# Regrouping the token blocks of an attention-plus-bilinear-FFN kernel: seven groups instead of eight, seven-product matmuls in five of them

## The chip, the cores and the metric

The kernel runs on one core of a Trainium2 chip. The metric is the device time of one execution in microseconds, the median of several runs. The engines of a core work side by side and wait for each other through semaphores: TensorE (PE in the profile; its weight loads are PEld), VectorE (DVE), ScalarE (ACT), GpSimd (POOL) and SyncE (SP), which here only issues transfers. GpSimd and ScalarE issue transfers too.

## The reference

Two layers are computed one after the other. The first is a causal linear attention with a decay per head, on q, k, v of shape (4 batches, 8 heads, 768 positions, 64). In blocks of the sequence it is

```
intra = einsum('bhic,bhjc->bhij', qb, kb) * Dmask      # lam ** (i - j), lower triangle
intra = einsum('bhij,bhjd->bhid', intra, vb)
inter = einsum('bhid,bhde->bhie', qb * lam_pow, kv_state)
out   = intra + inter
kv_state = lam_block * kv_state + einsum('bhsd,bhse->bhde', kb_dec, vb)
```

The second is a bilinear feed-forward layer on the 3072 tokens, x of shape (3072, 512): `a = x @ w_a`, `b = x @ w_b`, `out = (a * b) @ w_out`, with a hidden width of 1536. The output is (3072, 512) in float32.

## The kernel before

**Units and groups.** The 3072 tokens are cut into 24 units of 128 tokens, six to a batch. Attention is computed unit by unit, the feed-forward layer group by group: `GROUPS` (L28) lists how many units each group has. While TensorE runs the feed-forward matmuls of one group, the attention of the units of the next group is woven in between. The order of the weaving is written out by hand: `PLAN` lists, for each group, steps at numbered slots, and the feed-forward routine calls `hook(slot)` at fixed points of its own loop. The instructions are issued in exactly this program order on each engine. An engine works through its queue in order, so a step that waits holds up all that stands behind it on that engine.

**The steps of `PLAN`.** "P" prepares a unit (`prep_k`, L267): k is scaled by a decay vector (on VectorE for the first two units of group 1 on, else on GpSimd), q is scaled on GpSimd, the result is the bf16 tile `qk`; for units in `DMA_T` the SyncE queue then issues a DMA transpose of `qk` to `qkT`; at last `pump` issues the loads of q and k of later units on SyncE, up to a lookahead; then `make_vb` has GpSimd issue the load of v, cast to bf16 on the way. "T" is the transpose on TensorE (`piece_T`, eight 128-column matmuls and one ScalarE copy) for units that are not in `DMA_T`. "S" computes the scores and masks them on VectorE. "V" updates the running state (tile `kvd`) and copies it to SBUF. "O", "O2" and "Q" compute the attention output of one or two units ("Q" with the scores of two more) and copy it to `xT`, the feed-forward input. "W" stores a kept output row block. "TW" computes weight sums (`w_sums`, L467).

**The feed-forward layer.** A plain group (`ffn`, L613) computes, for each of 12 chunks of 128 hidden columns, four matmuls for a and four for b with as many columns as the group has tokens. ScalarE copies a to `a_sb`, VectorE multiplies it with b into `ab`. Then each unit takes twelve 512-column output matmuls (tile `op`). Group 0 is plain and runs the chunks as the weights arrive. A group in `S_GROUPS` runs `ffn_seven` (L492) instead. It treats the products as a 2-by-2 block problem and takes seven block products where the plain way takes eight, at the price of sums: sums of weight blocks `tw` (four VectorE subtractions for each of six parts of 256 hidden columns), sums of input blocks `xs`, and sums after the products, with ScalarE snapshots of PSUM (`s12`, `s5`, `u2`), VectorE sums (`c11`, `c12`, `c22`) and a GpSimd product into `ab`. `SUM_ON_VEC` lists the parts whose `c11` VectorE sums directly; for the others ScalarE copies and GpSimd sums. Before the change only groups of four units run it, and the part loop has six rounds of seven products with four 256-column matmuls each.

**Queues at the start.** SyncE loads q and k of the first four units; GpSimd issues the loads of v of these, then the weights in chunks, `wo_sb` last in six pieces. SyncE then waits, through tiny transfers into `landed`, for pieces 0, 3 and 5 of `wo_sb`, and issues q and k of units 4, 5 and 6 behind them. The load tiles `qf` and `kf` have three buffers each.

**Output.** Rows of the first `KEEP_GROUPS` groups are kept in SBUF and stored by "W" steps later; the others are stored at once. The last unit's output is split into three column ranges so that the last store is small.

Of the kernel before, what the change touches and what calls it, by code (L numbers as in the profile page):

```python
# [22 lines left out]
def _bc(ap, dims):  # L23
# [4 lines left out]
GROUPS = (4, 1, 2, 4, 4, 4, 4, 1)  # L28
# [3 lines left out]
LOOKAHEAD = {9: 2, 10: 1}  # L32
DMA_T = range(7, 24)
KEEP_GROUPS = 3
# [7 lines left out]
S_GROUPS = (3, 4, 5, 6)  # L42
SUM_ON_VEC = {3: (1, 2, 3, 4), 4: (2, 3, 4), 5: (2, 3, 4), 6: (1, 2, 3, 4)}
PLAN = {
    0: [(0, "V", 3), (7, "TW", (0, "dve")), (7, "TW", (1, "dve")), (23, "P", 4), (26, "T", 4),
        (29, "TW", (2, "dve")), (29, "TW", (3, "dve")), (29, "S", 4), (33, "O", 4), (35, "P", 5)],
    1: [(0, "V", 4), (2, "T", 5), (3, "P", 6), (6, "S", 5), (7, "T", 6), (10, "S", 6),
        (10, "TW", (4, "dve", (0,))), (10, "TW", (4, "dve", (1,))), (12, "O2", (5, 6)),
        (12, "TW", (4, "dve", (2,))), (13, "P", 7)],
    2: [(0, "V", 6), (1, "P", 8), (4, "P", 9), (7, "V", 7), (9, "S", 7), (9, "S", 8), (6, "P", 10),  # L50
        (10, "V", 8), (11, "Q", (7, 8, 9, 10)), (12, "P", 11), (12, "V", 9), (13, "O2", (9, 10)),
        (14, "P", 12)],
    3: [(1, "P", 13), (3, "P", 14), (11, "S", 11), (11, "S", 12),
        (7, "P", 15), (12, "P", 16), (14, "P", 17), (17, "P", 18)],
    4: [(6, "P", 19), (9, "P", 20), (13, "P", 21), (16, "P", 22)],
    5: [(6, "P", 23)],
    6: [(13, "O", 23)],
}
for _g, _u in ((3, 11), (4, 15), (5, 19)):
    PLAN[_g] += [(11, "V", _u), (13, "Q", (_u, _u + 1, _u + 2, _u + 3)), (14, "V", _u + 2),  # L60
                 (16, "O2", (_u + 2, _u + 3)), (18, "S", _u + 4)]
    if _g < 5:
        PLAN[_g] += [(19, "S", _u + 5)]
PLAN[3] += [(_s, "W", None) for _s in (9, 9, 9, 10, 10, 10, 10)]
PLAN[2] += [(_s, "TW", (4 + _n // 4, "dve", (_n % 4,)))
            for _n, _s in enumerate((2, 3, 5, 6, 12), 3)]
# [3 lines left out]
def kernel(  # L70
# [60 lines left out]
    def load_x(w, u):  # L131
        b, nb = divmod(u, NB)
        t = ld_pool.tile([128, H, D], F32, name=w + "f", tag=w + "f", bufs=3)
        nc.sync.dma_start(out=t, in_={"q": qr, "k": kr}[w][b, nb])
        raw[u, w] = t
# [31 lines left out]
    def pump():  # L167
        while pending:
            kind, c = pending[0]
            if kind == "after":  # L170
                nc.sync.dma_start(out=landed[:, c:c + 1], in_=wo_sb[0:1, 2 * c + 1, 0:1])
            elif c >= used["u"] + LOOKAHEAD.get(used["u"], 2 if used["u"] > 8 else 3):
                return
            else:
                load_x(kind, c)
            pending.pop(0)
# [76 lines left out]
    def make_ks(u, eng):  # L253
        qk = prep_pool.tile([128, 2, H, D], BF16, name="qk", tag="qk")
        scale(eng, qk[:, 1], raw.pop((u, "k")), lp_k[:, u % NB])
        U[u] = dict(qk=qk, kn=qk[:, 1])
# [10 lines left out]
    def prep_k(u):  # L267
        make_ks(u, "dve" if u < n0 + 2 else "pool")
        make_qs(u, "pool")
        used["u"] = u + 1  # L270
        if u in DMA_T:
            qkT = qkT_pool.tile([128, 2, HP, 128], BF16, name="qkT", tag="qkT")
            nc.sync.dma_start_transpose(
                out=qkT[:].rearrange("p j hp i -> p (j hp) i"),
                in_=U[u]["qk"][:].rearrange("p j h d -> p (j h d)"))
            U[u]["qT"], U[u]["kT"] = qkT[:, 0], qkT[:, 1]
        pump()
# [24 lines left out]
    def masks(u, kq):  # L302
        ms = mask(kq, split=u in (7, 8))
        U[u]["m"] = lambda i, hp: ms[i][:, hp, :]
# [103 lines left out]
    def pieces_O(us, nxt=()):  # L408
        kqs = [score_banks() for u in nxt]
        o_banks(us)  # L410
        for u, kq in zip(nxt, kqs):
            scores(u, kq)
        for u in us:
            inter(u)
        for b in range(2):
            for u in us:
                intra(u, b)
            evac_o(us, b)
        sums(us[-1])
        beside = len(us) == 2 and us[0] >= n0 + 5  # L420
        if beside:
            kv_beside(us[1])
        copy = beside and us[1] % NB < NB - 1
        for n, (u, kq) in enumerate(zip(nxt, kqs)):
            if n == 1 and copy:
                kv_copy(us[1], kv["ps"])
            masks(u, kq)
        if copy and len(nxt) < 2:
            kv_copy(us[1], kv["ps"])
# [37 lines left out]
    def w_sums(i, eng, which=range(4)):  # L467
        if i not in tw:
            tw[i] = wst_pool.tile([128, 4, 2, 256], BF16, name="tw", tag="wst")
        t = tw[i]  # L470
        e = nc.gpsimd if eng == "pool" else nc.vector
        c = slice(256 * i, 256 * i + 256)
        a1, a2, b1, b2 = wa_sb[:, 0:2, c], wa_sb[:, 2:4, c], wb_sb[:, 0:2, c], wb_sb[:, 2:4, c]
        for j in which:
            e.tensor_sub(t[:, j], *((b1, a1), (b2, t[:, 0]), (b2, b1), (a2, t[:, 1]))[j])

    def sums(u):
        g = next(i for i in range(len(GROUPS)) if g_u0[i] <= u < g_u0[i] + GROUPS[i])
        if g not in S_GROUPS or u != g_u0[g] + 3:
            return  # L480
        x = xTs[u][0]
        t = wst_pool.tile([128, 4, 2, 256], BF16, name="xs", tag="wst")
        x11, x12, x21, x22 = (x[:, k:k + 2, c:c + 256] for c in (0, 256) for k in (0, 2))
        nc.vector.tensor_add(t[:, 0], x22, x21)
        nc.vector.tensor_sub(t[:, 1], t[:, 0], x11)
        nc.vector.tensor_sub(t[:, 2], x11, x21)
        nc.vector.tensor_sub(t[:, 3], x12, t[:, 1])
        xs[g] = t
# [3 lines left out]
    def ffn_seven(g, u0, xT, hook):  # L492
# [4 lines left out]
        def bank_of(name):  # L497
            t = ps_bank(name, [128, 2, 256], F32, hold=True)
            return t, (bank["next"] - 1) % 7

        def product(i, ps, w, x, first):
            for f in range(2):
                for k in range(2):
                    nc.tensor.matmul(ps[:, f, :], lhsT=w(k, f), rhs=x[:, k, :],  # L504
                                     start=(first and f == 0 and k == 0), stop=True,
                                     skip_group_check=True)

        def w_of(w_sb, k0, i):
            return lambda k, f: w_sb[:, k0 + k, (2 * i + f) * 128:(2 * i + f + 1) * 128]

        def t_of(j, i):
            return lambda k, f: tw[i][:, j, k, f * 128:(f + 1) * 128]

        x11, x12, x22 = xT[:, 0:2, 0:256], xT[:, 2:4, 0:256], xT[:, 2:4, 256:512]

        def snap(name, ps, bufs, t=None):
            if t is None:
                t = sn_pool.tile([128, 2, 256], F32, name=name, tag=name, bufs=bufs)
# [3 lines left out]
        def step(i, n):  # L522
            d = live.setdefault(i, {})
            if n == 1:
                d["q"], d["qb"] = bank_of("m_q")
                product(i, d["q"], w_of(wa_sb, 0, i), x11, True)
                d["s12"] = wst_pool.tile([128, 2, 2, 256], F32, name="s12", tag="wst")
# [5 lines left out]
            elif n == 2:  # L533
                p, pb = bank_of("m_p")
                product(i, p, w_of(wa_sb, 2, i), x12, True)
                d["c11"] = a_pool.tile([128, 2, 256], BF16, name="c11", tag="a")
# [9 lines left out]
            elif n == 3:  # L546
                product(i, d["r"], w_of(wb_sb, 2, i), st[:, 3], False)
                c12 = sn_pool.tile([128, 2, 256], F32, name="c12", tag="c12", bufs=2)
                nc.vector.tensor_add(c12, d["u2"], d["r"])  # L549
                bank["held"].discard(d["rb"])  # L550
                nc.gpsimd.tensor_mul(ab[:, 2 * i:2 * i + 2, 0:256], d["c11"], c12)  # L551
            elif n == 7:
                product(i, d["q"], t_of(2, i), st[:, 2], False)
                d["c22"] = sn_pool.tile([128, 2, 256], F32, name="c22", tag="c22", bufs=1)
                nc.vector.tensor_add(d["c22"], d["s5"], d["q"])
            else:
                product(i, d["q"], t_of(3, i), x22, False)
                nc.vector.tensor_mul(ab[:, 2 * i:2 * i + 2, 256:512], d["c22"], d["q"])  # L558
# [4 lines left out]
        for i in range(FC // 2):  # L563
            for off, n in ((0, 1), (2, 5), (3, 2), (4, 6), (6, 3), (8, 7), (12, 4)):
                at[7 * i + off] = (i, n)
# [10 lines left out]
        out_mms(op, ab, 0, range(FC // 2))  # L576
        step(*at[end])
        hook(FC)
        out_mms(op, ab, 0, range(FC // 2, FC))
        store(u0, op, 0, d_model)  # L580
        hook(FC + 1)
        for t in range(1, 4):
# [30 lines left out]
    def ffn(u0, n, xT, hook, first, last):  # L613
# [25 lines left out]
        for t in range(n):  # L639
            op = ps_bank("op", [128, d_model], F32, ffn=True)  # L640
            if last and t == n - 1:
                for lo, hi in ((0, 256), (256, 384), (384, 512)):
                    if lo:
                        op = ps_bank("op", [128, d_model], F32, ffn=True)
                    out_mms(op, ab, t, range(FC), lo, hi)
                    store(u0 + t, op, lo, hi, nc.scalar if hi == d_model else None)
                return
# [114 lines left out]
    for c in range(FC // 2):  # L762
        load_w("o", c)
    for u in range(2):
# [27 lines left out]
    for g, n in enumerate(GROUPS):  # L792
# [6 lines left out]
        def hook(slot, plan=plan):  # L799
            for name, us in plan.get(slot, ()):  # L800
                if name == "P":
                    prep_k(us)
                    make_vb(us)
                elif name == "TW":
                    w_sums(*us)
# [15 lines left out]
        if g in S_GROUPS:  # L821
            ffn_seven(g, g_u0[g], gx.pop(g), hook)
        else:
            ffn(g_u0[g], n, gx.pop(g), hook, g == 0, g + 1 == len(GROUPS))
# [29 lines left out]
```

## Time and profile before

| | us |
|---|---|
| median of 7 runs | 223.85 (223.63 to 224.49) |
| profiled execution, device time | 223.8 |
| its span | 222.1 |
| TensorE busy | 215.3 (97%) |
| VectorE busy | 142.3 (64%) |
| GpSimd busy | 121.2 (55%) |
| ScalarE busy | 102.6 (46%) |

The granted TensorE clock is full throughout. By the order of time on TensorE, group 0 ends and group 1 begins at 50.95 us, group 2 begins at 61.80, group 3, the first with seven products, at 81.73, groups 4, 5 and 6 at 115.24, 148.6 and 181.3, and the last group of one unit at 210.93. The last output matmul ends at about 219.1.

A line of the timeline gives start, duration, engine, line, operation, output<-inputs, shapes and the count of merged instructions; a bracket tells how long the engine was idle before it and what ended that. Matmuls overlap, and their modelled durations are longer than the spacing of their starts; the spacing is what counts.

### The profile page before, as it was taken

What the parts mean: (1) busy time and instruction counts of PE and PEld (TensorE: products, weight loads), DVE (VectorE), ACT (ScalarE), POOL (GpSimd) and SP (SyncE); (2) the same over time, 40 slices, a digit from 0 to 9 for tenths busy, and PEclk for the clock granted to TensorE, in tenths of its full rate; (3) what the DMA queues carried; (4) which work ended last, traced back from release to release, by engine and by line L of the source; (5) the groups of instructions that cost most, each with busy time, mean ns of one, the idle gap of its engine ahead of it and who ended that gap; (6) DMA issues with size and microseconds to landing.
All of it is one profiled execution on the core that took longest, in us unless ns stands there. A gap on an engine that the chain in (4) does not pass through costs nothing.

```text
span 222.1 us, 5335 instructions
## 1 busy us (share of the span) xinstructions
PE 215.3 (97%) x2127; PEld 148.7 (67%) x2127; DVE 142.3 (64%) x251; ACT 102.6 (46%) x203; POOL 121.2 (55%) x135
## 2 busy tenths in 40 slices
PE   7699999999999999999999999999999999999994
PEld 2376444448788668886558885558886558884494
DVE  0991558394867977879485876385877367972050
ACT  2686223037444356562337561437562346552261
POOL 6589440376950948999438699607673006352000
PEclk9999999999999999999999999999999999999999
DMA  3999999999999497999999599991051110001211
GB/s 122 268 131 167 197 204 205 226 204 222 146 191 173 93 200 137 193 183 279 253 259 219 130 95 240 180 204 44 3 71 39 59 70 28 0 3 47 97 49 47
DMA packets 97550, 31.54 MB, mean 142 GB/s; under 512 B 85494, under 2 KB 94582, under 8 KB 97526
## 3 DMA queue, kind: packets, MB, share of 16 engines
q1 hardware_dynamic: 65334, 23.27, 46.4%
q0 software_dynamic: 31904, 7.87, 42.5%
q8 instruction: 16, 0.26, 0.5%
q10 hardware_dynamic: 288, 0.07, 0.1%
q14 instruction: 8, 0.07, 0.1%
HBM read 28.32 MB, written 6.29 MB: 156 GB/s over the span
## 4 chain that ended last, share of the span: by engine, by line
PE 70%; DMA 18%; POOL 4%; SPq 3%; issue 1%; ACT 1%; DVE 1%; POOLq 0%
PE op L610 23%; PE m_q L504 16%; PE m_r L504 8%; PE a_ps L438 5%; PE b_ps L438 5%; DMA wo_sb<-in_moe_w_out_dram 5%; PE o_ps L332 4%; PE m_p L504 4%; DMA qf<-in_q_dram 3%; DMA wa_sb<-in_moe_w_a_dram 3%; DMA vb<-in_v_dram 3%; DMA k<-in_k_dram 3%; PE kq L298 3%; DMA kf<-in_k_dram 2%; POOL ab L551 2%
## 5 line engine op out<-in xcount | busy, mean ns | idle before, releaser
L610 PE MATMUL op<-wo_sb,ab 128*128 128x512 bf16 (+2 forms) x312 | 67.4, 363 | 0.3 <-POOL ab L551 0.3
L610 PEld LDWEIGHTS <-ab 128*128 128x128 bf16 x312 | 27.9, 98 | 28.0 <-POOL ab L551 0.8
L504 PEld LDWEIGHTS <-tw 128*128 128x128 bf16 x384 | 37.5, 98 | 6.1
L465 DVE TENSOR_TENSOR ab<-a_sb,b_ps 128x128 bf16<-128x128 bf16 (+2 forms) x48 | 19.6, 420 | 27.9 <-ACT a_sb L447 16.1
L551 POOL TENSOR_TENSOR ab<-c,c 128x512 bf16<-128x512 bf16 x24 | 27.9, 1168 | 13.6 <-DVE c L549 13.1
L315 DVE TENSOR_TENSOR m<-kq,lotri 128x512 bf16<-128x512 f32 x45 | 28.5, 684 | 4.0 <-PE kq L298 3.4
L605 ACT COPY o_sb<-op 128x512 f32<-128x512 f32 (+2 forms) x19 | 10.3, 542 | 40.8 <-PE op L610 38.1
L504 PE MATMUL m_q<-xs,tw 128*128 128x256 bf16 x192 | 28.8, 272 | 0.0
L541 POOL TENSOR_TENSOR c<-s 128x512 bf16<-128x512 f32 x10 | 12.7, 1270 | 28.5 <-ACT s L519 28.4
L438 PE MATMUL b_ps<-xT,wb_sb 128*128 128x128 bf16 (+2 forms) x192 | 27.7, 272 | 0.0
L438 PE MATMUL a_ps<-xT,wa_sb 128*128 128x128 bf16 (+2 forms) x200 | 27.6, 268 | 0.0
L248 POOL TENSOR_TENSOR qk<-qf,lp_q 128x512 bf16<-128x512 f32 x20 | 20.8, 1039 | 10.5 <-DMA qf<-in_q_dram 10.5
L447 ACT CAST a_sb<-a_ps 128x128 bf16<-128x128 f32 (+2 forms) x48 | 17.4, 376 | 19.1 <-PE a_ps L438 18.6
L248 POOL TENSOR_TENSOR qk<-kf,lp_k 128x512 bf16<-128x512 f32 x18 | 18.8, 1044 | 12.1 <-DMA kf<-in_k_dram 9.7
L558 DVE TENSOR_TENSOR ab<-c,m_q 128x512 bf16<-128x512 f32 x24 | 16.5, 688 | 9.5 <-PE m_q L504 8.0
L264 POOL DMA_DIRECT2D vb<-in_v_dram x24 | 22.5, 940 | 0.0
L549 DVE TENSOR_TENSOR c<-u,m_r 128x512 f32<-128x512 f32 x24 | 16.4, 682 | 8.1 <-ACT u L519 8.1
L504 PEld LDWEIGHTS <-wa_sb 128*128 128x128 bf16 x192 | 18.6, 98 | 2.8
L438 PEld LDWEIGHTS <-wa_sb 128*128 128x128 bf16 x200 | 16.2, 98 | 6.2
L519 ACT COPY s<-m_q 128x512 f32<-128x512 f32 x24 | 14.1, 587 | 12.4 <-PE m_q L504 11.8
L438 PEld LDWEIGHTS <-wb_sb 128*128 128x128 bf16 x192 | 15.6, 98 | 6.1 <-DMA wb_sb<-in_moe_w_b_dram 0.4
L519 ACT COPY s<-m_r 128x512 f32<-128x512 f32 x24 | 14.1, 588 | 6.0 <-PE m_r L504 6.0
(81 smaller groups left out, 290.9 us busy)
## 6 DMA issues: line engine op xcount, KB each, us to landing
qf<-in_q_dram SPq DMA_DIRECT2D x20, 256.0 KB, 4.7
kf<-in_k_dram SPq DMA_DIRECT2D x20, 256.0 KB, 5.1
out_dram<-o_sb SPq DMA_DIRECT2D x16, 256.0 KB, 2.0
vb<-in_v_dram POOLq DMA_DIRECT2D x24, 128.0 KB, 5.4
out_dram<-o_kept SPq DMA_DIRECT2D x7, 256.0 KB, 4.9
wa_sb<-in_moe_w_a_dram POOLq DMA_DIRECT2D x6, 256.0 KB, 7.6
wb_sb<-in_moe_w_b_dram POOLq DMA_DIRECT2D x6, 256.0 KB, 8.1
wo_sb<-in_moe_w_out_dram POOLq DMA_DIRECT2D x6, 256.0 KB, 10.2
```

What stands on the lines that cost most here:

```text
L248: eng_of(eng).tensor_mul(dst.rearrange("p (c b) d -> p b c d", b=2), x[:].rearrange("p (b c) d -> p b c d", b=2), lp.rearrange("p (b c) o ...
L264: nc.gpsimd.dma_start(out=vb, in_=vr[b, nb])
L315: nc.vector.tensor_mul(m, kq[i], lotri_bc)
L438: nc.tensor.matmul(ps[:, lo:hi], lhsT=w_sb[:, s, f * 128:(f + 1) * 128], rhs=xT[:, s, lo:hi], start=(s == 0), stop=(s == KS - 1), skip_gro ...
L447: nc.scalar.copy(a_sb[:, :gt], ps[:, :gt])
L465: nc.vector.tensor_mul(ab[:, f, :gt], a_sb[:, :gt], ps[:, :gt])
L504: nc.tensor.matmul(ps[:, f, :], lhsT=w(k, f), rhs=x[:, k, :], start=(first and f == 0 and k == 0), stop=True, skip_group_check=True)
L519: nc.scalar.copy(t, ps)
L549: nc.vector.tensor_add(c12, d["u2"], d["r"])
L551: nc.gpsimd.tensor_mul(ab[:, 2 * i:2 * i + 2, 0:256], d["c11"], c12)
L558: nc.vector.tensor_mul(ab[:, 2 * i:2 * i + 2, 256:512], d["c22"], d["q"])
L610: nc.tensor.matmul(op[:, lo:hi], lhsT=ab[:, f, t * 128:(t + 1) * 128], rhs=wo_sb[:, f, lo:hi], start=(f == 0), stop=(f == FC - 1))
```

## The change

The groups become 4, 2, 4, 4, 4, 4, 2 units. Group 0 now prepares two units (4 and 5) instead of one; the one-unit groups are gone. The last five groups, the last one of two units among them, run `ffn_seven`; for this the routine is generalised: with `n` units the half width is `h = n * 64` and a round covers `nf = 512 / h` chunks, so that the last group has three rounds of seven products with eight 128-column matmuls each. `out_last` splits the last unit's output there. All six weight-sum parts are computed on VectorE in group 0, at slots 4, 6, 9, 11, 14 and 18. Unit 6 is transposed by DMA. The scaling of k runs on VectorE for units 4 to 9 (before: 4 and 5). The load tiles have four buffers, the lookahead is three units throughout, and the loads of v for units 4 and 5 are issued by GpSimd behind pieces 3 and 5 of `wo_sb`. Rows of the first two groups (six units) are kept.

```diff
-GROUPS = (4, 1, 2, 4, 4, 4, 4, 1)
+GROUPS = (4, 2, 4, 4, 4, 4, 2)
...
-LOOKAHEAD = {9: 2, 10: 1}
-DMA_T = range(7, 24)
-KEEP_GROUPS = 3
+DMA_T = range(6, 24)
+KEEP_GROUPS = 2
...
-S_GROUPS = (3, 4, 5, 6)
-SUM_ON_VEC = {3: (1, 2, 3, 4), 4: (2, 3, 4), 5: (2, 3, 4), 6: (1, 2, 3, 4)}
+S_GROUPS = (2, 3, 4, 5, 6)
+SUM_ON_VEC = {2: (0, 1, 2, 3, 4), 3: (2, 3, 4), 4: (2, 3, 4), 5: (1, 2, 3, 4), 6: (0, 1, 2)}
 PLAN = {
-    0: [(0, "V", 3), (7, "TW", (0, "dve")), (7, "TW", (1, "dve")), (23, "P", 4), (26, "T", 4),
-        (29, "TW", (2, "dve")), (29, "TW", (3, "dve")), (29, "S", 4), (33, "O", 4), (35, "P", 5)],
-    1: [(0, "V", 4), (2, "T", 5), (3, "P", 6), (6, "S", 5), (7, "T", 6), (10, "S", 6),
-        (10, "TW", (4, "dve", (0,))), (10, "TW", (4, "dve", (1,))), (12, "O2", (5, 6)),
-        (12, "TW", (4, "dve", (2,))), (13, "P", 7)],
-    2: [(0, "V", 6), (1, "P", 8), (4, "P", 9), (7, "V", 7), (9, "S", 7), (9, "S", 8), (6, "P", 10),
-        (10, "V", 8), (11, "Q", (7, 8, 9, 10)), (12, "P", 11), (12, "V", 9), (13, "O2", (9, 10)),
-        (14, "P", 12)],
...
+    0: [(0, "V", 3), (4, "TW", 0), (6, "TW", 1), (9, "TW", 2), (11, "TW", 3), (14, "TW", 4),
+        (18, "TW", 5), (23, "P", 4), (26, "T", 4), (27, "P", 5), (28, "S", 4), (30, "T", 5),
+        (31, "V", 4), (32, "S", 5), (34, "O2", (4, 5)), (35, "P", 6)],
+    1: [(1, "P", 7), (3, "P", 8), (6, "P", 9), (7, "S", 6), (8, "V", 6), (9, "S", 7), (11, "O2", (6, 7)),
+        (12, "S", 8), (12, "V", 8), (13, "S", 9), (13, "P", 10), (14, "O2", (8, 9)), (15, "P", 11)],
...
-        t = ld_pool.tile([128, H, D], F32, name=w + "f", tag=w + "f", bufs=3)
+        t = ld_pool.tile([128, H, D], F32, name=w + "f", tag=w + "f", bufs=4)
...
-            elif c >= used["u"] + LOOKAHEAD.get(used["u"], 2 if used["u"] > 8 else 3):
+            elif c >= used["u"] + 3:
...
     def prep_k(u):
-        make_ks(u, "dve" if u < n0 + 2 else "pool")
+        make_ks(u, "dve" if u < n0 + 6 else "pool")
...
-def ffn_seven(g, u0, xT, hook):
+def ffn_seven(g, u0, n, xT, hook, last):
+        h = n * BLK // 2
+        nf = 512 // h
...
-        out_mms(op, ab, 0, range(FC // 2))
+        early = FC // 2 if nf == 2 else FC - nf
+        out_mms(op, ab, 0, range(early))
         step(*at[end])
         hook(FC)
-        out_mms(op, ab, 0, range(FC // 2, FC))
+        out_mms(op, ab, 0, range(early, FC))
...
+            if last and t == n - 1:
+                out_last(u0 + t, ab, t)
+                return
...
     for c in range(FC // 2):
         load_w("o", c)
+        if c in (3, 5):
+            make_vb(n0 + (c - 3) // 2)
...
                 if name == "P":
                     prep_k(us)
-                    make_vb(us)
+                    if us > n0 + 1:
+                        make_vb(us)
```

## The prediction

> **What bounds the kernel now.** I read the engine shares first, then the slices, then the waits of TensorE, then the instructions in order of time around the change.
>
> ```profile
> PE 215.3 (97%) x2127; PEld 148.7 (67%) x2127; DVE 142.3 (64%) x251; ACT 102.6 (46%) x203; POOL 121.2 (55%) x135
> PE   7699999999999999999999999999999999999994
> DVE  0991558394867977879485876385877367972050
> DMA  3999999999999497999999599991051110001211
> ```
>
> TensorE is full from the fourth slice to the last but one, so its matmul count sets the time wherever nothing is late. Modelled matmul ends overlap, so the share proves little; the waits do: after 17 us TensorE waits 0.2 us for `vb` and 0.3 us for an `ab`, nothing else. A matmul taken away is thus worth its issue time, and a new wait is paid in full. The data side is nearly as tight up to 75 us (DMA row at nines), and the chain of waits runs through it exactly where the change works:
>
> ```profile
> 35.49 6.76 DMA qf<-in_q_dram
> 42.33 0.99 POOL qk L248
> 43.32 6.36 DMA vb<-in_v_dram
> 49.73 0.41 PE o_ps L332 x8
> ```
>
> Unit 4's q lands at 42.3, its v at 49.7, and TensorE takes it 0.05 us later: group 0's end has no slack. The timeline of the engines there:
>
> ```profile
> 37.30 0.69 DVE L465 TENSOR_TENSOR ab<-a_sb,b_ps 128x512 bf16<-128x512 bf16 x1 [0.17 <-PE b_ps L438]
> 39.03 0.69 DVE L465 TENSOR_TENSOR ab<-a_sb,b_ps 128x512 bf16<-128x512 bf16 x1 [0.17 <-PE b_ps L438]
> 43.15 0.77 DVE L248 TENSOR_TENSOR qk<-kf,lp_k 128x512 bf16<-128x512 f32 x1 [3.43 <-DMA kf<-in_k_dram]
> 43.84 0.41 DVE L475 TENSOR_TENSOR tw<-wb_sb,wa_sb 128x512 bf16<-128x512 bf16 x1
> 44.28 1.36 DVE L475 TENSOR_TENSOR tw<-wb_sb,tw 128x512 bf16<-128x512 bf16 x1
> ...
> 44.29 1.06 POOL L248 TENSOR_TENSOR qk<-qf,lp_q 128x512 bf16<-128x512 f32 x1
> ...
> 45.24 0.61 PE L284 MATMUL tps<-ident,qk 128*128 128x128 bf16 x8
> 45.68 1.46 PE L610 MATMUL op<-wo_sb,ab 128*128 128x512 bf16 x6
> 47.07 0.40 PE L298 MATMUL kq<-qkT 64*128 64x128 bf16 x8
> ...
> 50.95 0.39 PE L438 MATMUL a_ps<-xT,wa_sb 128*128 128x128 bf16 x4
> 51.17 0.39 PE L438 MATMUL b_ps<-xT,wb_sb 128*128 128x128 bf16 x4
> ```
>
> To be seen: VectorE is idle from 39.7 to 43.15, scales unit 4's k as it lands (the `qk<-kf` row), and TensorE transposes the unit at 45.24. A weight sum takes 0.41 us, but 1.36 when GpSimd's q scaling runs beside it.
>
> **TensorE's work: a gain of 1.8 us.** Four 128-column matmuls take 0.222 us (50.95 to 51.17), 55.5 ns each. Counting the built programs: 192 such matmuls of the two one-unit groups go, 168 of the last group's seven products come (3 rounds x 7 x 8), and the two-unit group and the four full groups keep theirs. 24 x 55.5 ns = 1.33 us. Unit 6's eight transposes go: 8 x 55.5 = 0.44. Smaller: four more score blocks issued singly (0.33 us, against 0.55 for a pair, so +0.2), two single attention outputs become pairs (0.62 against 0.46 each, -0.3), one more start of the seven-product pipeline (its first products slip by 0.17 at 81.7 us, +0.2), the 0.18 us wait for `vb` goes. Sum -1.8.
>
> A rule speaks against this part. The Trainium skill, "TensorE: Matmul & The Clock Gate", section Back-to-back issue gap, gives 81 ns a matmul for a sustained stream of 128 columns with a weight load each. By it the last group costs 168 x 81 = 13.6 us, more than two units done plainly with 256 columns (96 x 109 ns = 10.5). By the row, whose every matmul has its weight load too, it is 9.3. I use the row; both ends for the matmuls: -1.3 and +3.0 (9.3 becomes 13.6).
>
> In the last group each round still gives ScalarE three copies (0.59) and VectorE four operations (0.69), 2.75 us beside 3.1 us of TensorE. The last products are covered: eight output matmuls (1.73) stand ahead of the one that waits for `c22`, and 2.6 us stand between the last `c12` input and the output matmuls that need GpSimd's product (0.2+0.68+1.17+0.2 = 2.25). Cost nothing; without that cover 0.5 us. The split last store is the same.
>
> **Weight sums: a wait of 2.3 us at unit 4's transpose.** In the built order all 24 sums stand on VectorE ahead of unit 4's k scaling; before, 8 did. Nothing reorders VectorE's queue. The sums of parts 0 and 1 (4 x 0.375 = 1.5 us each; eight took 3.0 at 32.7) fall into its 1.9 us pauses: free; with no pause they would hold banks by 1.5. From the product of chunk 9, paced by TensorE at 37.30: 0.6, sums of part 2 1.5, two products 1.2, parts 3 to 5 4.5 = 45.1 us. GpSimd scales q of units 4 and 5 inside this stretch (q4 lands at 42.3; q5, issued at 40.1 and 3.9 us on its way, at 44.0 or later), and each takes about 0.95 us from a sum (1.36 less 0.41): between nothing and 1.9; I take 1.5, as the two may overlap only in part. k4 starts at 46.65, not 43.15, is ready at 47.35, the transpose comes at 47.5: 2.3 us late (0.7 to 2.8). Nothing of TensorE can pass it: output matmuls, scores and attention are queued behind it in order.
>
> **What is late next in group 0.** Two units, not one, are now prepared inside it, with less between. A transpose to its score took 1.83 us (45.24 to 47.07) through ScalarE's 1.01 us copy, covered by six output matmuls; now four stand there (0.45+0.87): 0.5 more. For unit 5 four output matmuls and a state update (0.45+1.09): 0.3. At the end two output matmuls (0.43) stand between the attention output and the first product of group 1, which needs two copies of 512 columns (1.07 in the pair row); ScalarE is done at about 1.1: 0.65. Together 1.45 (0.5 to 2). `vb` of units 4 and 5 is issued behind output-weight loads 3 and 5, so 0.94 us each of GpSimd's issue, inside its idle time after 31.8, and some 1.3 us each on the transfers (256 KB at 200 GB/s). Loads 4 and 5 come to 41 and 43.5, needed at 48 and later; q6 waits behind load 5 on SP for 1.3 us more, needed after 54. Hidden, and unit 4's own v stops being the end of the chain.
>
> **Group 1: 0.8 us.** k scaling of units 6 to 9 moves to VectorE, where it stands in order behind the products of group 1, so a transfer's transpose can no longer run ahead. With group 1 at 55.6: unit 6 is scaled at 54.7, its DMA transpose issued on SP at 54.8 and landed 5.5 to 6.8 later (row of the tile), needed at 62.6: hidden. Unit 7 is scaled behind the second product, 58.6, landed 64.2 to 65.4, needed at 64.9: 0 to 0.5. Unit 8: needed 69.7, there at 68. Unit 9: its k is issued on SP behind unit 6's transpose at 57, lands about 63, VectorE reaches it at 62.3 and stands still for about 0.7, with seven products, six masks and two state copies queued behind; TensorE runs on by its banks, then loses some of it at the outputs of units 6 and 7. Its transpose lands by 71, needed 71.5. I take 0.4 + 0.4; ends 0 and 5, as unit 9's chain has the least margin and in the trace three transposes took SP 8.5 us. The relief: GpSimd is rid of four scalings of 1.04 us, off the path.
>
> **The rest.** Fourth load buffers and the even lookahead bring loads earlier; the full groups ran 33.3 us each with no wait on transfers, so nothing. Kept stores: six instead of seven, off the path. With six sums out of groups 1 and 2 VectorE is lighter there; TensorE did not wait for it: nothing, -0.3 at best.
>
> **Sum.** -1.8 + 2.3 + 1.45 + 0.8 = +2.75 us. The profiled execution took 223.8 us, span 222.1 (1.7 around it), and the median is 223.85, so the same offset serves: span 224.9, median 226.6.
>
> **Rivals.** (1) Faster: k4 is not held up. If the transpose waits under 0.3 us and the copies after it are covered, only the removed matmuls count: 222.1. For it: VectorE had 3.4 us free before k4. Against: 16 more sums are 6 us. The change gains only if the waits of group 0 and group 1 stay together under 1.35 us, that is k4 ready by about 45.8 with the scalings of q costing nothing. (2) DMA transposes become the bound in group 1: unit 9's arrives 3 to 5 us late, and the masks behind it; 230. For it: DMA at nines until 75 us and a transpose that blocks SP up to 3.0 us. Against: the waits of group 0 give transfers that much more time. (3) The seven products on two units run at the rule's pace or wait on evacuations: 4.3 more, 230 with the rest. Against: the row above. (4) The waits and the removed work cancel: sums uncontended and half the copies covered, 223.8.
>
> **How the numbers follow.** My forecast 0.62 (224.6 to 228); rival 1 0.15; rivals 2 and 3 0.08 and 0.05; rival 4 0.10. Of the forecast nothing is under 224.3; rival 4 is split, 0.07 within 0.2% and 0.03 above. (0.2%, about 0.45 us, is what a measurement of this kernel tells from no change.) So faster 0.15, same 0.07, slower 0.78. Range 223.1 to 228.6: below lies most of rival 1, above rivals 2 and 3.
>
> **What would show it.** In the trace after: k4 scaled on VectorE at 46 to 47 right behind a weight sum; the `tps` rows with a wait for VectorE of about 2 us; group 1's first `a_ps` at 55 to 56 (51.9 with no wait); the last group 9.3 us of 128-column products; score rows of units 7 and 9 waiting under 1 us for `qkT`. Wrong if k4 is scaled at 43 to 44, if the seven products of the last group show gaps, or if group 2 starts much later than group 1 plus 21.5 us.

## The result and the profile after

The changed kernel takes 225.25 us in the median (223.88 to 228.76), the kernel before, run on the same chip, 223.73: a ratio of 1.0073, with a 95% interval of 1.0056 to 1.0090. It is slower by 1.5 us. The profiled execution took 224.55 us with a span of 222.8, against 223.8 and 222.1 before: the trace shows 0.7 us of loss and is itself 0.7 us under the median. The longest of the 24 executions, 228.76 us, had a mean granted clock of 0.992; eight others above 226 us had 0.998 or more. What those did was not recorded. So the trace tells where a short execution loses time, and the medians of the experiments tell how much a part of the change is worth; the 0.7 us between the two stay unexplained.

From the page of the changed kernel, its shares and the slices that answer to those of before:

```profile
PE 215.8 (97%) x2099; PEld 146.7 (66%) x2099; DVE 146.1 (66%) x250; ACT 99.7 (45%) x182; POOL 117.5 (53%) x131
PE   7899999989999999999999999999999999999994
DVE  0991685965796788893678773578773598730760
DMA  4999999999999999999960999300911200012102
```

TensorE has 28 instructions fewer (x2099 against x2127), and its busy time is not lower (215.8 us against 215.3). Modelled matmul ends overlap, so the share doesn't show what was saved; the waits show what was lost. The only new gap in TensorE's row is the 8 in the ninth slice, 44.6 to 50.1 us, the end of group 0. The timeline of that stretch (start, duration, engine, line, operation; in brackets the idle time before it and what ended it):

```profile
43.84 0.42 DVE L464 TENSOR_TENSOR tw<-wb_sb,tw 128x512 bf16<-128x512 bf16 x1
43.92 1.25 POOL L240 TENSOR_TENSOR qk<-qf,lp_q 128x512 bf16<-128x512 f32 x1 [9.50 <-DMA qf<-in_q_dram]
44.18 1.26 DVE L465 TENSOR_TENSOR tw<-wb_sb 128x512 bf16<-128x512 bf16 x1
45.22 0.40 PE L276 MATMUL tps<-ident,qk 128*128 128x128 bf16 x4
...
45.70 0.68 DVE L240 TENSOR_TENSOR qk<-kf,lp_k 128x512 bf16<-128x512 f32 x1
46.44 0.40 PE L276 MATMUL tps<-ident,qk 128*128 128x128 bf16 x4 [0.82 <-DVE qk L240]
47.94 0.40 PE L290 MATMUL kq<-qkT 64*128 64x128 bf16 x8 [0.24 <-ACT qkT L278]
...
53.60 0.87 PE L430 MATMUL a_ps<-xT,wa_sb 128*128 128x256 bf16 x4
```

These rows are the last of the sums; VectorE runs them without a pause until it scales unit 4's k, called k4 from here on, at 45.70 (before: at 43.15, after an idle stretch of 3.43 us). One sum of the last part, beside GpSimd's scaling of q, took 1.26 us instead of 0.42. TensorE has transposed q's half at 45.22 and waits for k's. But group 1 begins at 53.60, not at the 55.6 predicted.

The table adds up how far TensorE's starts lie apart beyond the plain spacing of the instruction between them (128 columns 55.5 ns, 256 columns 109 ns, 512 columns 216 ns):

| place | extra us in the trace | predicted |
|---|---|---|
| unit 4's transpose | 1.0 | 2.3 |
| unit 4's score, unit 5's score | 0.40, 0.18 | 0.5, 0.3 |
| first product of group 1 | 0.26 | 0.65 |
| rest of group 1 | 0.3 | 0.8 |
| first products of group 2 | 0.46 | not named |
| sum | 2.6 | 4.55 |

TensorE's last matmul ends 0.8 us later than before (219.93 against 219.1). 0.8 - 2.6 = -1.8 us is left for the removed work, which is what the prediction counted. That is a rest, not a measurement, and good to some 0.3 us: the table leaves out one more wait of 0.30 for `ab` than before, and part of its last row (0.17 of 0.46) was lost before too, at the first seven products. The experiment on the last group below measures the largest part of the rest.

The last row of the table, in the timeline at the start of group 2:

```profile
72.95 1.03 POOL L240 TENSOR_TENSOR qk<-kf,lp_k 128x512 bf16<-128x512 f32 x1 [1.13 <-DMA kf<-in_k_dram]
73.54 0.73 DVE L476 TENSOR_TENSOR xs<-xT 128x512 bf16<-128x512 bf16 x1 [1.92 <-ACT xT L347]
73.96 1.21 POOL L240 TENSOR_TENSOR qk<-qf,lp_q 128x512 bf16<-128x512 f32 x1
74.31 1.15 DVE L477 TENSOR_TENSOR xs<-xs,xT 128x512 bf16<-128x512 bf16 x1
75.51 0.33 PEld L498 LDWEIGHTS <-tw 128*128 128x128 bf16 x4 [0.34 <-DVE xs L477]
```

Unit 12 is scaled on GpSimd (the two POOL rows) while VectorE makes the sums of x that the seven products need. Two of them take 0.73 and 1.15 us; the two behind them, alone, take 0.41 each. The first products that need them wait.

The loads explain the rest of the first stretch. From the view of the tile `kf` in the changed kernel, the time from issue to landing over all units:

```profile
DMA to landing us min/median/max: 4.1/5.0/9.7
```

The maximum is unit 4's k: issued at 35.78, it was 9.7 us on its way and landed at 45.5. Before, it took 7.2 us. Unit 4's q took 8.5 us instead of 6.8. What was issued ahead of them now, from GpSimd's queue, are the v loads of units 4 and 5, from the timeline of the changed kernel:

```profile
29.70 0.88 POOL L256 DMA_DIRECT2D vb<-in_v_dram  x1 [0.58 <-DMA wa_sb<-in_moe_w_a_dram]
...
33.55 0.87 POOL L256 DMA_DIRECT2D vb<-in_v_dram  x1 [0.59 <-DMA wb_sb<-in_moe_w_b_dram]
```

Before, they were issued at 43.32 and 45.28, behind the loads of k4 and of unit 4's q (q4). So k4 landed 0.2 us before the sums let VectorE go: two causes meet at one moment, and taking away either one alone should show little.

### The profile page after: what moved, and what is told of

The parts are those of the page before. It is cut to its first block, busy times and chain, and to the rows that moved or that the text cites. A ratio compares the mean times of both kernels' runs of the same rounds, so it can differ in the third digit from the quotient of the medians.

```text
span 222.8 us, 5228 instructions
## 1 busy us (share of the span) xinstructions
PE 215.8 (97%) x2099; PEld 146.7 (66%) x2099; DVE 146.1 (66%) x250; ACT 99.7 (45%) x182; POOL 117.5 (53%) x131
## 4 chain that ended last, share of the span: by engine, by line
PE 55%; DMA 15%; POOL 15%; SPq 5%; DVE 3%; issue 3%; ACT 2%; POOLq 0%; ACTq 0%
PE op L608 21%; PE m_q L498 14%; PE m_r L498 7%; POOL ab L545 5%; DMA wo_sb<-in_moe_w_out_dram 4%; POOL qk L240 4%; DMA wb_sb<-in_moe_w_b_dram 4%; PE o_ps L324 4%; PE m_p L498 4%; SPq L126 3%; DMA k<-in_k_dram 3%; DMA kf<-in_k_dram 2%; PE kq L290 2%; POOL vb L256 2%; DMA qf<-in_q_dram 2%
## 5 line engine op out<-in xcount | busy, mean ns | idle before, releaser
L498 PEld LDWEIGHTS <-tw 128*128 128x128 bf16 x480 | 43.2, 98 | 6.4 <-DVE xs L477 0.3
L498 PE MATMUL m_q<-xs,tw 128*128 128x256 bf16 (+1 forms) x240 | 32.4, 262 | 0.1
L498 PEld LDWEIGHTS <-wa_sb 128*128 128x128 bf16 x240 | 21.5, 98 | 2.9
L457 DVE TENSOR_TENSOR ab<-a_sb,b_ps 128x512 bf16<-128x512 bf16 (+1 forms) x24 | 13.0, 549 | 13.4 <-PE b_ps L430 13.3
L532 DVE TENSOR_TENSOR c<-s,m_p 128x512 bf16<-128x512 f32 x18 | 12.4, 687 | 11.1 <-PE m_p L498 11.0
L439 ACT CAST a_sb<-a_ps 128x512 bf16<-128x512 f32 (+1 forms) x24 | 11.4, 479 | 17.5 <-PE a_ps L430 16.6
L549 DVE TENSOR_TENSOR c<-s,m_q 128x512 f32<-128x512 f32 x27 | 18.5, 685 | 0.5
L430 PE MATMUL a_ps<-xT,wa_sb 128*128 128x256 bf16 (+1 forms) x104 | 18.4, 314 | 0.3
L430 PE MATMUL b_ps<-xT,wb_sb 128*128 128x512 bf16 (+1 forms) x96 | 18.4, 326 | 0.0
L513 ACT COPY u<-m_q 128x512 f32<-128x512 f32 x27 | 16.0, 593 | 5.3 <-PE m_q L498 5.3
```

Of the source, the lines that this page charges most:

```text
L430: nc.tensor.matmul(ps[:, lo:hi], lhsT=w_sb[:, s, f * 128:(f + 1) * 128], rhs=xT[:, s, lo:hi], start=(s == 0), stop=(s == KS - 1), skip_gro ...
L457: nc.vector.tensor_mul(ab[:, f, :gt], a_sb[:, :gt], ps[:, :gt])
L513: nc.scalar.copy(t, ps)
```

## Experiments

The first question is which of the two, sums or early v loads, holds up k4; then whether the removed matmuls are worth what they were counted at; then what the scaling of k on VectorE and the start of group 2 cost. Ratios are to the kernel before on the same chip, with a 95% interval.

### The changed kernel again

> The changed kernel once more, unedited, for a second traced execution beside the other runs. Its executions spread over some 3 us (223.9 to 227.2) where those of the kernel before mostly keep within 1.5. Theory D (late transfers make the spread): the span differs from 222.8 by what TensorE waits at unit 4's and 5's transposes and at the scores of units 6 to 9 (1.0, 0, 0.1, 0.2 us in the first trace). Theory P (the spread is spread evenly over all groups): the full groups, 33.4 us each in the first trace, differ too. Median 225.2.

Measured: 224.83 us, ratio 1.0060 (1.0039 to 1.0082), span 222.8. Unit 4's transpose waited 0.27 for q and 0.57 for k, the score behind it 0.24, and the full groups ran as in the first trace. The waits in group 0 repeat; the loss is 1.1 to 1.5 us. This trace is of a short execution too, so neither theory of the spread is settled.

### The last part's sums moved to group 1

```diff
     0: [(0, "V", 3), (4, "TW", 0), (6, "TW", 1), (9, "TW", 2), (11, "TW", 3), (14, "TW", 4),
-        (18, "TW", 5), (23, "P", 4), (26, "T", 4), (27, "P", 5), (28, "S", 4), (30, "T", 5),
+        (23, "P", 4), (26, "T", 4), (27, "P", 5), (28, "S", 4), (30, "T", 5),
...
     1: [(1, "P", 7), (3, "P", 8), (6, "P", 9), (7, "S", 6), (8, "V", 6), (9, "S", 7), (11, "O2", (6, 7)),
+        (11, "TW", 5),
```

> Weight sums of part 5 moved from slot 18 of group 0 to slot 11 of group 1, so that they no longer stand ahead of unit 4's k scaling. Theory S (the sums hold k4 up, as predicted): k4 is scaled at 43.9 instead of 45.7, the transpose of unit 4 no longer waits 1.0 us, time 224.2. Theory V (the v loads placed among the output weights hold k4's landing up): k4 still lands at 45.5, the transpose still waits 0.8 to 1.0 us, time unchanged at 225.2.

Measured: 225.02 us, ratio 1.0063 (1.0042 to 1.0084): no change against the changed kernel. VectorE is now free in time and waits for the load instead; the timeline of this kernel:

```profile
43.47 0.42 DVE L467 TENSOR_TENSOR tw<-wa_sb,tw 128x512 bf16<-128x512 bf16 x1
46.13 0.69 DVE L241 TENSOR_TENSOR qk<-kf,lp_k 128x512 bf16<-128x512 f32 x1 [2.24 <-DMA kf<-in_k_dram]
46.88 0.40 PE L277 MATMUL tps<-ident,qk 128*128 128x128 bf16 x4 [0.87 <-DVE qk L241]
```

The sums end at 43.8, VectorE idles for 2.24 us, and TensorE waits as long as before. With the early v loads in place the sums are not what decides.

### The v loads of units 4 and 5 back in the preparation of the unit

```diff
-        if c in (3, 5):
-            make_vb(n0 + (c - 3) // 2)
...
-                    if us > n0 + 1:
-                        make_vb(us)
+                    make_vb(us)
```

> The loads of v of units 4 and 5 go back to where the kernel before has them, in the units' own preparation; the sums stay. Theory V: k4 lands at 43.2 again instead of 45.5, but the sums end at 45.4 all the same, so unit 4's transpose gains 0.1 to 0.3 us only. Theory S says the same of it. Against it v of unit 4 lands at about 50 and v of unit 5 at 52 to 53, wanted at 50.0 and 52.5: 0 to 1 us of new waits. Time 225.0 to 226.

Measured: 226.93 us, ratio 1.0129 (1.0092 to 1.0166): slower than the changed kernel by 1.7 us. The loads come early (k4 after 7.2 us, at 42.7), and so GpSimd scales q of units 4 and 5 in the midst of the sums. The timeline of this kernel:

```profile
41.94 1.15 POOL L240 TENSOR_TENSOR qk<-qf,lp_q 128x512 bf16<-128x512 f32 x1 [10.52 <-DMA qf<-in_q_dram]
42.22 1.15 DVE L464 TENSOR_TENSOR tw<-wb_sb,tw 128x512 bf16<-128x512 bf16 x1
43.96 1.39 DVE L463 TENSOR_TENSOR tw<-wb_sb,wa_sb 128x512 bf16<-128x512 bf16 x1
...
46.40 2.13 DVE L240 TENSOR_TENSOR qk<-kf,lp_k 128x512 bf16<-128x512 f32 x2
47.99 0.61 PE L276 MATMUL tps<-ident,qk 128*128 128x128 bf16 x4 [2.63 <-DVE qk L240]
```

Two sums are stretched to 1.15 and 1.39 us, k4 comes at 46.40 and the transpose at 47.99, 2.6 us late. This is the mechanism of the prediction, with nearly its numbers (46.65, 47.5, 2.3), in a kernel without the early v loads. One part of the 2.6 is not the prediction's: k4's own scaling met a third scaling of q (of unit 6) and took 1.56 us instead of 0.68. The early v loads lengthen k4's way by 2.5 us and spare VectorE two of these three collisions; on balance they help.

The wait then cost more than its length. Windows of 2 us of this kernel (columns: the window and its length, the busy time of PE, PEld, DVE, ACT and POOL with their instructions, then the granted TensorE clock, where 1.00 is full, a DMA column and GB/s):

```profile
46.00:48.00 2.00, 0.01 (x1) 0.01 (x1) 2.00 (x4) 0.00 (x0) 1.87 (x2) 0.93 1.79 214
48.00:50.00 2.00, 2.00 (x8) 0.85 (x8) 0.54 (x1) 1.01 (x1) 1.47 (x3) 0.50 1.63 179
50.00:52.00 2.00, 2.00 (x17) 0.95 (x17) 1.12 (x2) 0.00 (x0) 0.73 (x1) 0.71 1.72 233
```

Behind the pause the clock is at half for two microseconds and below full in the next window. In the traces the span grew by 2.4 us against the changed kernel and the wait by 1.8. The executions bear it out: four of the six had a mean clock of 0.992 and took 226.87 to 227.85 us; the two at full clock took 224.63 and 225.83, no more than the changed kernel. How long TensorE waited in those two was not recorded.

### Both: sums of the last part and v loads late

The two edits above together.

> Both: sums of part 5 in group 1 and v of units 4 and 5 in their preparation. If sums and v loads hold k4 up to the same moment, only both together bring it back: k4 scaled at 43.2 to 44, transpose of unit 4 at 45.2 with no wait, 1.0 us less there; new waits for v of 0 to 1.5 us as TensorE comes earlier. Theory S alone: the same as the run with the sums moved. Time 224.2 to 225.5.

Measured: 224.92 us, ratio 1.0048 (1.0032 to 1.0065). k4 is scaled at 43.94, unit 4's transpose waits for nothing, and group 1 begins at 52.34, 1.26 us earlier than in the changed kernel. Two rows of its timeline:

```profile
43.94 0.68 DVE L241 TENSOR_TENSOR qk<-kf,lp_k 128x512 bf16<-128x512 f32 x1
...
44.83 0.61 PE L277 MATMUL tps<-ident,qk 128*128 128x128 bf16 x8
```

Either cause alone is thus enough to make the transpose wait; only with both gone did the wait go (0.31 and 0.35 us of it came back in two later kernels with the same two edits, where scalings of q fell differently). But most of the gain is given back in the trace: the scores of units 7 and 9 are 0.36 and 0.37 late, held by the transfers that transpose them, and the first products of group 2 wait longer, 1.1 us against 0.46. The timeline there:

```profile
73.33 1.22 POOL L241 TENSOR_TENSOR qk<-kf,lp_k 128x512 bf16<-128x512 f32 x1 [2.06 <-DMA kf<-in_k_dram]
...
74.52 1.21 POOL L241 TENSOR_TENSOR qk<-qf,lp_q 128x512 bf16<-128x512 f32 x1
74.75 1.26 DVE L480 TENSOR_TENSOR xs<-xT,xs 128x512 bf16<-128x512 bf16 x1
76.07 0.61 PE L499 MATMUL m_r<-xs,wb_sb 128*128 128x256 bf16 x4 [0.95 <-DVE xs L480]
```

Group 2 starts earlier, unit 12's load does not, and its two scalings again fall on sums of x, now on the last two, of which the last is waited for.

### Both v loads behind the last output-weight load, the last sums in group 1

```diff
-        if c in (3, 5):
-            make_vb(n0 + (c - 3) // 2)
+        if c == 5:
+            make_vb(n0)
+            make_vb(n0 + 1)
```

> Sums of part 5 in group 1, and both v loads behind the last piece of the output weights instead of between pieces. Theory V: k4 lands at 43.2 to 44 and v of unit 4 by 45, so unit 4's transpose waits for nothing and the state update for nothing: group 1 starts at 52.1 instead of 53.6. Theory G (what group 0 gains is given back): TensorE then waits 0.7 us for the DMA transposes of units 7 and 8 and about 1 us for the input sums at the start of group 2, as in the run with both moved; time 224.5. Without giving back, 223.5.

Measured: 224.98 us, ratio 1.0053 (1.0030 to 1.0077), span 224.1. k4 was still 9.8 us on its way (45.2) and the transpose waited 0.68. For k4 it is not the place among the output weights that counts, it is that the v loads stand ahead of it at all; q4 took 7.8 us, between the 6.8 and 8.5 of the others. In this trace the scores of units 7 and 9 waited 1.32 and 0.46 for their transposing transfers, which in the changed kernel they did not: their slack is sometimes used up.

### A longer wait at the same place

```diff
-        (18, "TW", 5), (23, "P", 4), (26, "T", 4), (27, "P", 5), (28, "S", 4), (30, "T", 5),
+        (18, "TW", 5), (18, "TW", 5), (23, "P", 4), (26, "T", 4), (27, "P", 5), (28, "S", 4), (30, "T", 5),
...
```

The second pass writes the same sums into the same tile.

> The four sums of the last weight part are computed twice in a row, 1.5 us more on VectorE ahead of unit 4's k; nothing else changes. k4 is scaled 1.5 us later, at about 47.5, and TensorE waits 2.4 us at unit 4's transpose instead of 0.8 to 1.0. If a wait costs only its length: 225.25 + 1.5 = 226.7. Theory of the clock: a pause of over 2 us is followed by some 3 us at half clock, as in the kernel with the late v loads (2.63 us wait, clock 0.50 right behind it), so 1.5 us more: about 228, mean clock 0.992 in the profile and slices of 0.5 to 0.7 behind the pause.

Measured: 227.68 us, ratio 1.0174 (1.0148 to 1.0200), span 226.1, mean clock 0.992 in every execution. The wait was 3.12 us, 2.3 longer and not 1.5, because the added sums met a second scaling of q. Group 1 begins at 57.02, 3.4 us later than in the changed kernel. Timeline and windows of this kernel:

```profile
48.39 0.40 PE L276 MATMUL tps<-ident,qk 128*128 128x128 bf16 x4 [3.12 <-DVE qk L240]
48.62 1.03 PE L610 MATMUL op<-wo_sb,ab 128*128 128x512 bf16 x4
50.43 1.89 PE L610 MATMUL op<-wo_sb,ab 128*128 128x512 bf16 x4
52.12 1.06 PE L276 MATMUL tps<-ident,qk 128*128 128x128 bf16 x8
```

```profile
48.00:50.00 2.00, 1.37 (x12) 0.65 (x14) 1.78 (x2) 1.01 (x1) 2.00 (x2) 0.92 1.21 274
50.00:52.00 2.00, 2.00 (x12) 0.81 (x11) 1.29 (x2) 0.00 (x0) 1.83 (x3) 0.50 0.96 176
52.00:54.00 2.00, 2.00 (x17) 1.42 (x15) 0.11 (x1) 0.79 (x1) 1.93 (x3) 0.73 1.51 159
```

The four output matmuls that took 1.03 us at 48.62 take 1.89 at 50.43, and eight transposes 1.06 instead of 0.61. The extra spacing in the slow stretch is 0.21 (unit 4's score) + 0.83 + 0.41 + 0.07 (the next outputs) = 1.5 us on top of the wait. The clock part of the expectation is shown in the trace, and there the sum closes: 2.3 us of wait and 1.5 of clock are 3.8; TensorE reached the transpose 0.33 us earlier than in the changed kernel (44.89 against 45.22), and groups 1 and 2 lost 0.1 less; the span grew by 3.3. The medians can't separate the two parts: they are 2.4 us apart, 2.9 with the second timing of the changed kernel.

### The last group with plain products

```diff
-S_GROUPS = (2, 3, 4, 5, 6)
+S_GROUPS = (2, 3, 4, 5)
```

with the split last store passed on to the plain form.

> The last group of two units done plainly: 96 matmuls of 256 columns in place of 168 of 128, the rest as in the changed kernel. By the count at the rates of the first traces (109 and 55.5 ns) the group takes 10.5 instead of 9.3 us: 1.1 us slower than the changed kernel beside it, 226.0 where that is 224.9. If 128-column matmuls with a weight load each really went at 81 ns it would be 3 us faster. If the sums after the products hold TensorE up at the end, it loses less than 1.

Measured: 225.90 us, ratio 1.0107 (1.0089 to 1.0126), span 223.7. The first products of the last group and the outputs behind them, first in the changed kernel, then in this one:

```profile
205.08 0.61 PE L498 MATMUL m_q<-xT,wa_sb 128*128 128x128 bf16 x8
...
214.08 1.89 PE L608 MATMUL op<-wo_sb,ab 128*128 128x512 bf16 x8
215.81 0.61 PE L498 MATMUL m_q<-xT,tw 128*128 128x128 bf16 x8
216.25 3.68 PE L608 MATMUL op<-wo_sb,ab 128*128 128x512 bf16 x40
```

```profile
204.49 0.60 PE L430 MATMUL a_ps<-xT,wa_sb 128*128 128x256 bf16 x4
...
214.97 5.40 PE L608 MATMUL op<-wo_sb,ab 128*128 128x512 bf16 x48
```

168 products of 128 columns take 216.25 - 205.08 less the eight outputs among them (1.73): 9.4 us, 56 ns each. 96 plain ones of 256 columns take 10.5. The difference of 1.0 in the traces (1.1 counted) stands against 0.7 in the medians (1.1 against the second timing of the changed kernel). The seven products gain; at the 81 ns each of the rule that the prediction quotes they would have lost 3.1.

### Unit 6 transposed on TensorE again

```diff
-DMA_T = range(6, 24)
+DMA_T = range(7, 24)
...
-    1: [(1, "P", 7), (3, "P", 8), (6, "P", 9), (7, "S", 6), (8, "V", 6), (9, "S", 7), (11, "O2", (6, 7)),
+    1: [(1, "P", 7), (3, "P", 8), (5, "T", 6), (6, "P", 9), (7, "S", 6), (8, "V", 6), (9, "S", 7), (11, "O2", (6, 7)),
```

> One part of the change undone: unit 6 is transposed on TensorE again (slot 5 of group 1), not by DMA. By the step of the prediction (eight transposes, 8 x 55.5 ns, a part of a TensorE that is full) this kernel is 0.44 us longer than the changed kernel: 225.25 becomes 225.7, ratio to before about 1.008. If the DMA transpose only moved the cost (a queue held up, units 7 to 9 later), the time stays at 225.2 or falls. In the trace: eight more tps products at about 58 us, and the score of unit 6 right behind its copy on ScalarE.

Measured: 225.45 us, ratio 1.0081 (1.0055 to 1.0107). The sign is as expected, +0.2 us where 0.44 was counted, but the intervals hold both 0.44 and nothing. The transposes stand at 59.29, the score right behind them finds its copy, and the wait at unit 4 is the 0.82 of the changed kernel. Inconclusive as to size.

### k of units 6 to 9 scaled on GpSimd again

```diff
-        make_ks(u, "dve" if u < n0 + 6 else "pool")
+        make_ks(u, "dve" if u < n0 + 2 else "pool")
```

> k of units 6 to 9 scaled on GpSimd again, as before, the rest as in the changed kernel. Prediction's theory (k scaling in VectorE's order makes units 7 and 9 late in group 1): 0.3 to 0.8 us faster, the score rows of units 6 to 9 with no wait for their transposes. Theory C (the chain of transfers, not VectorE, sets those): unchanged within 0.4, as the first trace shows 0.3 us of waits in all of group 1.

Measured: 224.42 us, ratio 1.0036 (1.0023 to 1.0049), span 222.5. Unit 4's transpose waits 0.82 as before, so group 0 is untouched; group 1 runs as in the changed kernel, and at the start of group 2 the first products lose 0.17 us instead of 0.46. The move of the k scaling costs the changed kernel 0.4 to 0.8 us (against its two medians).

### Unit 12 prepared one slot later

First on the kernel with both v loads behind the last output weights and the last sums in group 1:

```diff
-    2: [(1, "P", 12), (4, "P", 13), (7, "P", 14), (11, "S", 10), (11, "S", 11), (12, "P", 15),
+    2: [(2, "P", 12), (4, "P", 13), (7, "P", 14), (11, "S", 10), (11, "S", 11), (12, "P", 15),
```

> The same, and unit 12's preparation one slot later, behind GpSimd's first product of group 2, so that its scalings no longer run beside VectorE's input sums at the start of that group. Theory G with the collision as its second half: the 1.1 us wait of the first m_r row goes, time 1 us below the run without it, about 223.5. If the sums are late for another reason (ScalarE's copies), unchanged.

Measured: 223.96 us, ratio 1.0028 (1.0012 to 1.0043), against 1.0053 without this edit. The sums of x take 0.42 us each and nothing waits at the start of group 2, although unit 4's transpose waited 1.65 in this trace. The trace without this edit had lost only 0.3 there, so most of the 1.0 us between the two medians is not this wait, and stays open. The wait of 1.65 and a window over its end, with the clock at full:

```profile
46.65 0.40 PE L277 MATMUL tps<-ident,qk 128*128 128x128 bf16 x4 [1.65 <-DVE qk L241]
46.00:48.00 2.00, 1.26 (x8) 0.53 (x8) 0.59 (x1) 0.92 (x1) 0.72 (x1) 1.00 0.76 172
```

Then the same edit on the kernel with both parts late:

> The v loads behind the output weights and the last sums in group 1, as in the kernel of two late parts (224.92), and the preparation of unit 12 one slot later in group 2, so that GpSimd's scaling of unit 12 no longer stands beside the xs sums; k of units 6 to 9 stays on VectorE. Theory of the collision at the start of group 2: the 1.1 us wait at its m_r products goes and nothing else changes: 223.8, ratio about 1.000; xs sums 0.42 each. If the wait there was only the relaxation of an earlier lateness (unit 9's masks, say), the time stays at 224.9.

Measured: 224.00 us, ratio 1.0001 (0.9982 to 1.0021), against 1.0048. By both pairs, as ratios and as medians, one slot of one unit's preparation is worth 0.6 to 1.1 us in these kernels, and the last one is level with the kernel before. Its timeline:

```profile
70.15 0.40 PE L291 MATMUL kq<-qkT 64*128 64x128 bf16 x8 [1.06 <-DMA qkT<-qk]
...
73.79 0.42 DVE L477 TENSOR_TENSOR xs<-xT 128x512 bf16<-128x512 bf16 x1 [1.92 <-ACT xT L348]
...
74.92 0.42 DVE L480 TENSOR_TENSOR xs<-xT,xs 128x512 bf16<-128x512 bf16 x1
```

The collision is gone, and with it the 1.1 us of the kernel with both parts late. The score of unit 9 now waits 1.06 us for its transposing transfer in this execution, which took 0.4 us more than the median of this kernel.

### Both late, and k of units 6 to 9 on GpSimd

The edits of both late parts and of k on GpSimd together. (Where the expectation has unit 8 waiting for its transfer, it was unit 9.)

> Three edits on the changed kernel: the v loads of units 4 and 5 behind the output weights again, the last part's sums in group 1, and k of units 6 to 9 scaled on GpSimd. Theory: the matmuls' gain of about 1.3 to 1.8 us is real and is eaten by the wait at unit 4's transpose (1.0) and by the collisions on VectorE at the start of group 2 (up to 1.1). With both gone the kernel beats the one before: 223.0 to 223.5, ratio 0.996 to 0.999; no wait at unit 4's transpose, group 1 starts at 52.3, group 2 at about 72.5, its m_r products without a wait. Rival: something else in groups 0 and 1 gives the gain back whatever is moved (DMA transposes of units 7 and 8, which waited 0.7 when only the first two edits were made): 224.4 or more.

Measured: 224.99 us, ratio 1.0063 (1.0043 to 1.0082): a miss by 1.5 us or more. The gains of the two edits do not add. The timeline of this kernel:

```profile
44.10 2.26 DVE L241 TENSOR_TENSOR qk<-kf,lp_k 128x512 bf16<-128x512 f32 x2
45.82 0.40 PE L277 MATMUL tps<-ident,qk 128*128 128x128 bf16 x4 [0.35 <-DVE qk L241]
...
72.83 1.32 DVE L477 TENSOR_TENSOR xs<-xT 128x512 bf16<-128x512 bf16 x1 [1.74 <-ACT xT L348]
...
74.21 0.61 PE L499 MATMUL m_r<-xs,tw 128*128 128x256 bf16 x4 [0.34 <-DVE xs L477]
```

k4 is scaled early but beside unit 5's q on GpSimd, and is done in about 1.7 us instead of 0.7; the sums of x meet unit 12's scalings again. Both collisions came back, each at another instruction. The trace shows 0.5 and 1.0 us of extra spacing at these places; why the median is another 0.6 us over the traced execution stays open. No version beat the kernel before. Not tried: unit 12 a slot later in the changed kernel itself, or together with k on GpSimd; and nothing undoes the four load buffers, the even lookahead or the kept rows, so the prediction's zero for these is untested.

## Why the prediction was right, and where it was off

Forecast 226.6 us, slower, with 223.1 to 228.6; measured 225.25. The side is right, and the traces bear out the reason given for it: new waits, the largest at unit 4's transpose, take more than the removed matmuls bring. The size was nearer than its terms. In the traced execution the span grew by 0.7 us where +2.75 was summed up; that the median is only 1.35 under the forecast owes to the 0.7 us by which it lies above the trace, which nobody forecast. Of the five signs named for the trace, the last group's 9.3 us and the scores of units 7 and 9 came; k4 at 46 to 47 (45.70), the wait of about 2 us (0.82) and group 1 at 55 to 56 (53.60) did not.

- **TensorE's work, -1.8.** Held as far as it was measured. The last group took 9.4 us where 9.3 was counted, and making it plain cost 0.7 to 1.1 where 1.1 was. The rule of 81 ns a matmul (the Trainium skill, "TensorE: Matmul & The Clock Gate", section Back-to-back issue gap) doesn't hold for these products, with a weight load each: 56 ns. What unit 6's transposes are worth is not shown: the sign came as expected, inside the noise.
- **A wait of 2.3 at unit 4's transpose.** The place and the engine were right; 1.0 was measured. The step that failed is "some 1.3 us each on the transfers ... Hidden": it charged the early v loads to output-weight loads 4 and 5 and to unit 6's q, and put nothing for q4 and k4, which are issued after them too. These were delayed by 1.7 and 2.5 us on their way, as undoing the v loads showed; 2.5 is about two of the prediction's 1.3. With q4 late, GpSimd met one sum (0.84 us) instead of the 1.5 us of collisions taken, so the sums let VectorE go at 45.70 and not 46.65; and k4 would not have been there sooner. Undoing the v loads brought out nearly the predicted numbers (k4 at 46.40, a wait of 2.63), in part by chance: about 0.9 us of that wait is k4's own scaling beside GpSimd, which the prediction did not have.
- **What is late next in group 0, 1.45.** Mis-sized: 0.84, by the same copies through ScalarE. Most of the difference is at the first product of group 1, 0.26 against 0.65.
- **Group 1, 0.8.** The size is about right by chance, the place wrong. Units 7 and 9 waited for no transfer in the traces of the changed kernel, and group 1 lost 0.3. The other part came at the first products of group 2, where VectorE's sums of x and GpSimd's scaling of unit 12 collide; "the full groups ... so nothing" passed over it. Moving unit 12 by a slot was worth 0.6 to 1.1 us in two of the edited kernels.
- **Rivals.** Rival 1 (k4 in time) asked that the waits of groups 0 and 1 stay under 1.35 together; they are 2.1, and 2.6 with group 2. The kernel with both parts late removed the wait at k4 and still was not faster than before. Rival 2 (transposing transfers) did not show in the changed kernel, but did, on units 7 and 9 as the prediction named them, by 0.4 to 1.3 us in all three of the kernels in which group 1 started earlier and these scalings stayed on VectorE. Rival 3 is refuted by the last group, rival 4 (a cancellation to 223.8) did not occur.

## What to carry to other kernels

Where work is put on an engine in order ahead of a step with a due time, count the engine's queue, the landing of the step's data and what another engine does beside it; here two of these came to the same moment, and taking one away alone changed nothing or made it worse. A load that was issued earlier was paid for by loads issued after it, though from another queue. And a wait that is removed brings the next instructions earlier against work that did not move: look for what they will then stand beside.

## What the hardware showed that was not expected

- **The clock after a pause.** A pause of TensorE of 2.63 us was followed by about 3.4 us at a clock of 0.50 on balance (from the windows: 0.07 + 0.50 + 0.29 of 2 us each are 1.7 us lost; some 0.3 us of the slow stretch lie in the pause itself), a pause of 3.12 us by the same (0.08 + 0.50 + 0.27). In the second case the outputs at 48.62 still ran at full pace (1.03 us): by the windows the half clock came over a microsecond after TensorE had resumed. Behind waits of 0.82 and 1.65 us the windows show 1.00. The Trainium skill ("TensorE: Matmul & The Clock Gate", Part 1) gives about 3.4 us of idling as what halves the clock, and about as long to regain it; the second part agrees, but the shorter pause was enough here, and the measurement decides.
- **VectorE beside GpSimd.** A sum of two bf16 tiles takes 0.42 us alone and 0.73 to 1.39 when a scaling on GpSimd runs beside it; a scaling of k on VectorE, 0.68 alone, took 1.56. GpSimd's own scaling mostly grows only from 1.04 to 1.25. So most of the price is paid on VectorE, and once for each scaling that falls into a run of sums; the placing of one unit's preparation moved the kernel by up to 1.1 us.
- **Loads in another queue.** Two v loads of GpSimd's queue, issued at 29.7 and 33.6 instead of 43.3 and 45.3, lengthened the way of unit 4's k on SyncE's queue from 7.2 to 9.7 us. It repeats: 7.2 in all five traces with the v loads late, 9.7 to 9.9 in all nine with them early, wherever among the output-weight loads they stood.
